# One 7.9 MB load with its last 16 rows taken as sixteen one-row loads from GpSimd's queue

## The chip, the cores and the metric

The kernel runs on one core of a Trainium2 chip. The metric is the device time of one execution in microseconds (us). Two runs of the kernel before gave 711.76 and 711.79 us, median 711.77.

## What is computed

One decode step of two layers, run twice over the same weights and caches: attention with a residual, then an MLP with a residual, each after a layer norm. In short:

```python
def reference(A_x, A_k_cache, A_v_cache, A_wq, A_wo, B_x, B_w1, B_w2):
    x = A_x                                   # 4 x 1 x 640
    for _ in range(2):
        x = x + _A_ref(_layernorm(x), A_k_cache, A_v_cache, A_wq, A_wo)
        x = x + _B_ref(_layernorm(x), B_w1, B_w2)
    return x
```

`_A_ref` is attention with 32 heads of 128 over the last 1024 positions of the caches: q = x wq, softmax of q k / sqrt(128), the weighted sum of v, then wo. `_B_ref` is relu(x w1) w2 with 1728 hidden columns. The batch is 4, with one token each. Everything is float32.

## The kernel before, in words

All weights and caches are read from memory in both rounds (r = 0 and r = 1 in the code), some 302 MB in all, and hardly any of it is used twice. So the host packs the input into rows that are read in long runs. For each of the 32 heads there is a record of REC = 9472 columns over 128 partitions: 640 columns of wq (WQ), 4096 of K, 4096 of V and 640 of wo (WO). Row p of the array `rec` holds the records of all heads one after another, so a load of any stretch of columns is 128 long runs, one for each partition.

On the chip the tile `slots` holds NS = 5 records side by side, and `ring` holds the weights of the MLP and one more record. In round one the heads run in order, and head h lies in slot h % 5.

The order of the loads is written out by hand. `items` (from line 174) lists every load with its source columns and its place. `stream` (line 191) takes the records of five heads as one stretch and cuts it in three, at the columns of CUTS (line 55): 0, 15744, 31616 and 47360. `pump` (line 247) issues the next loads of the list on SP's queue, as long as the columns that they overwrite have been given free; `done` (line 278) gives columns free once the matmuls that read them have been written down, and calls `pump`. The waits on the chip follow from that: a load waits on the last matmul that reads the old content. Each engine's instructions are kept in the order of the program by `InOrder` (line 80).

For head h of round one the program runs: `scores` of the next head on TensorE (PE), `softmax` on VectorE (DVE) and ScalarE (ACT), `values` of this head (PE), `picks` (DVE), `query` of the head after the next (PE), `output_T` and `project` of this head (PE and ACT), `weights` (DVE). The loop stands at lines 512 to 531.

The load that the change touches is the second cut of the group of heads 10 to 14. Its first part is named ("rec", 0, 11). It holds head 11 from its column 6272 on (the rest of V, and WO), all of head 12, and head 13 up to its column 3200 (wq and part of K). It is 15872 columns wide, 63,488 bytes a row. The load before it in the list is the first cut of the same group, the one after it the third cut, and then follows the first cut of heads 15 to 19.

GpSimd (POOL) runs a few instructions that set up constants at the start, and nothing after. ACT issues the four small loads of x at the start (line 141); all other loads are issued by SP.

Of the kernel before, what the change touches and what calls it, by code (L numbers as in the profile page):

```python
# [2 lines left out]

# [11 lines left out]
P = 128  # L40
# [34 lines left out]
W1_SLOT = [[0, 1], [2], [3], [4]]  # L75
W2_SLOT = [22, 14, 10, 4, 4]
LATE = 5


class InOrder:  # L80
# [21 lines left out]
def decode_kernel(ctx: ExitStack, tc: tile.TileContext, xf, rec, w, out):  # L102
    nc = tc.nc
    pe, dve, act, pool, sp = (InOrder(tc, e) for e in (nc.tensor, nc.vector, nc.scalar, nc.gpsimd, nc.sync))
# [11 lines left out]
    hT = scratch.rearrange("p (m j) -> p m j", j=32)  # L116
    oTs = sb.tile([P, LATE, B], F32, name="oTs")
    qT = sb.tile([P, B], F32, name="qT")
# [59 lines left out]
    buffers = {"slots": slots, "ring": ring}  # L178
# [8 lines left out]
    def piece(r, h, lo, hi, buf=None, col=None):  # L187
        buf, col = place(home(h, r) if buf is None else buf, lo if col is None else col)
        items.append(([(("rec", r, h), lo, hi, col)], rec, h * REC + lo, h * REC + hi, buf, col))
# [9 lines left out]
    def ending(r, hs, late):  # L199
# [4 lines left out]
        if late:  # L204
            for h in hs[-1:] + hs[-LATE:-1]:
                piece(r, h, WO, REC)
# [8 lines left out]
    for h in hs[5 * NS:-3]:  # L215
        piece(0, h, 0, RING if h == SIXTH else WO if h >= H - LATE else REC)
    piece(0, SIXTH, RING, REC, "ring", 0)
# [29 lines left out]
    def pump():  # L247

        while items:
            parts, src, lo, hi, buf, col = items[0]  # L250
            if any(b == buf and x < col + hi - lo and col < y for b, x, y in live):
                return
            sp.dma_start(buffers[buf][:, col:col + hi - lo], src[:, lo:hi])
            live.append((buf, col, col + hi - lo))
            for key, x, y, c in parts:
                at.setdefault(key, []).append((x, y, buf, c))
            items.pop(0)
# [20 lines left out]
    def done(key, lo, hi):  # L278

        if key[0] == "rec" and key[1] == 0 and key[2] >= LAST:  # L280
            return
        if key == ("rec", 0, SIXTH):
            hi = min(hi, HELD)
        for x, y, buf, col in pieces(key):
            a, b = col + max(lo, x) - x, col + min(hi, y) - x
            if a < b:
                free(buf, a, b)
        pump()
# [5 lines left out]
    def put_by():  # L294

        for col, a, b in held:
            dve.tensor_copy(hold[:, col:col + b - a], ring[:, a:b])
            free("ring", a, b)
        free("ring", BESIDE, KEPT)
        pump()  # L300

    def lend():

        act.activation(*lent, AF.Copy)
        free("ring", HELD, BESIDE)
        pump()
# [193 lines left out]
    for r in range(2):  # L500
        hs = order[r]
        late = LATE if r == 0 else 2
        if r == 0:
# [8 lines left out]
        for n, h in enumerate(hs[:-2]):  # L512
            i = n - (H - late)
# [82 lines left out]
```

## Time and profile before

| | us |
|---|---|
| median of two runs | 711.77 |
| the profiled execution, its own span | 710.5 |
| PE busy | 513.6 (72%) |
| DVE busy | 323.3 (46%) |
| ACT busy | 99.7 (14%) |
| GpSimd busy | 1.1 |
| share of the 16 DMA engines' span that SP's queue fills | 99.1% |
| mean rate of the DMA | 426 GB/s |

The profile is of one execution. PE is the matmul unit, PEld its weight loads, SP the engine that issues the loads; "SPq" and "ACTq" are the issuing instructions. "slots<-rec" is a load from the array `rec` into the tile `slots`, "acc", "o_ps" and "sc_ps" are tiles in PSUM that matmuls write. A helper (line 94) issues nearly every instruction, so groups are told apart by their tiles and not by their lines. In the parts on the DMA, a packet is one run of bytes that one DMA engine moves, or one completion mark of 4 bytes; a stretch of time counts a packet whole where it starts, so that the share of a short stretch can be over 100%. The queue q1 is SP's, q10 is ACT's; those called "instruction" fetch the program. A row of the chain of waits has its start, its length, and what it is.

### The profile page before, as it was taken

Reading aid. Unit: us, or ns where it says so; the run is one execution under the profiler, and the core shown is the slowest. Engines: PE = TensorE matmul, PEld = TensorE weight load, DVE = VectorE, ACT = ScalarE, POOL = GpSimd, SP = SyncE. Lnnn points to the kernel's source line nnn. Section 1 sums busy time; section 2 is a strip of 40 time slices with the busy share of each in tenths; the row PEclk is TensorE's granted clock in tenths of the full one; section 3 lists DMA queues with packets and bytes.
Section 4 is the critical chain, followed back from the end, with each engine's and each line's share of the span. In section 5 each row is a group of like instructions: output and inputs, shape, how many; then the busy total and the mean of one; then the engine's idle time right before and its main releaser. Section 6 shows DMA issues by size and latency. Waiting matters only on the chain.

```text
span 710.5 us, 8690 instructions
## 1 busy us (share of the span) xinstructions
PE 513.6 (72%) x3706; PEld 202.8 (29%) x3706; DVE 323.3 (46%) x678; ACT 99.7 (14%) x211; POOL 1.1 (0%) x9
## 2 busy tenths in 40 slices
PE   3567686678584578857888898865686677576897
PEld 2132232232231223322223334331331322231423
DVE  3333353353452353546641777644352444253762
ACT  1100110011010110111121212201010111011111
POOL 0000000000000000000000000000000000000000
PEclk9957787677777776888999899977576677677899
DMA  9999999999999999999999999999999999999997
GB/s 381 463 409 451 415 442 443 414 442 444 424 429 440 434 429 421 435 425 430 424 416 403 421 435 428 438 434 448 429 445 427 428 442 430 427 442 406 431 423 292
DMA packets 13318, 302.64 MB, mean 426 GB/s; under 512 B 1488, under 2 KB 1760, under 8 KB 5216
## 3 DMA queue, kind: packets, MB, share of 16 engines
q1 hardware_dynamic: 13248, 302.08, 99.1%
q8 instruction: 29, 0.48, 0.2%
q14 instruction: 9, 0.07, 0.0%
q10 hardware_dynamic: 32, 0.01, 0.0%
HBM read 302.00 MB, written 0.08 MB: 425 GB/s over the span
## 4 chain that ended last, share of the span: by engine, by line
DMA 73%; PE 21%; DVE 4%; issue 1%; ACT 1%; SPq 0%; ACTq 0%; DVEq 0%
DMA slots<-rec 57%; PE sc_ps L94 11%; DMA ring<-w 8%; PE o_ps L94 7%; DMA ring<-rec 5%; PE acc L94 2%; DMA slots<-w 2%; DVE scratch L94 2%; DVE o_ps L94 1%; ACT oTs L94 1%; DVE small L94 0%; ACT sc_ps L94 0%; DVE turned L94 0%; SPq L94 0%; DVE ring L94 0%
## 5 line engine op out<-in xcount | busy, mean ns | idle before, releaser
L94 PE MATMUL sc_ps<-slots,qT 128*4 128x512 f32 x992 | 194.5, 869 | 37.4 <-DMA slots<-rec 36.4
L94 PE MATMUL sc_ps<-xT,slots 128*128 128x4 f32 x620 | 94.6, 279 | 99.8 <-DMA slots<-rec 99.2
L94 PE MATMUL o_ps<-slots,scratch 128*16 128x512 f32 x960 | 149.3, 693 | 2.4 <-DVE scratch L94 1.7
L94 DVE TENSOR_REDUCE small<-sc_ps 128x1 f32<-128x1024 f32 x64 | 78.3, 1224 | 156.9 <-PE sc_ps L94 156.9
L94 PEld LDWEIGHTS sc_ps<-xT,slots 128*128 128x128 f32 x620 | 89.2, 225 | 157.8 <-DMA slots<-rec 109.0
L94 ACT ACTIVATE sc_ps<-sc_ps,small 128x1024 f32<-128x1024 f32 (+1 forms) x68 | 71.1, 1046 | 342.2 <-DVE small L94 340.7
L94 DVE STREAM_TRANSPOSE turned<-sc_ps 128x1024 f32<-128x1024 f32 (+1 forms) x85 | 84.6, 996 | 0.7
L94 PEld LDWEIGHTS o_ps<-slots,scratch 128*16 128x16 f32 x960 | 34.5, 118 | 120.0 <-issue 107.6
L94 DVE TENSOR_TENSOR o_ps<-o_ps,of_block 128x512 f32<-128x512 f32 x62 | 43.4, 699 | 53.6 <-PE o_ps L94 52.3
L94 PEld LDWEIGHTS sc_ps<-slots,qT 128*4 128x4 f32 x992 | 32.3, 108 | 121.9 <-issue 64.9
L94 DVE TENSOR_TENSOR qT<-sc_ps,by_row 128x4 f32<-128x4 f32 x62 | 9.7, 156 | 114.1 <-PE sc_ps L94 114.1
L94 PE MATMUL acc<-slots,oTs 128*4 128x160 f32 x496 | 35.4, 368 | 19.2 <-ACT oTs L94 18.5
L94 DVE TENSOR_REDUCE scratch<-o_ps 128x128 f32<-128x512 f32 x62 | 42.9, 691 | 2.1
L94 ACT ACTIVATE oTs<-o_ps 128x4 f32<-128x4 f32 x64 | 11.1, 174 | 214.1 <-PE o_ps L94 214.1
L94 PE MATMUL o_ps<-pick,scratch 128*128 128x4 f32 x128 | 26.8, 280 | 15.9 <-DVE scratch L94 15.9
L94 PEld LDWEIGHTS o_ps<-pick,scratch 128*128 128x128 f32 x128 | 22.4, 218 | 21.4 <-DVE scratch L94 21.1
L94 DVE TENSOR_TENSOR scratch<-turned,by_row 128x128 f32<-128x128 f32 (+1 forms) x85 | 22.0, 259 | 3.2
L94 PE MATMUL sc_ps<-slots,small 128*1 128x512 f32 (+2 forms) x56 | 21.5, 486 | 0.0
L94 DVE TENSOR_SCALAR by_row<-of_batch,small 128x4 f32<-128x4 f32 x64 | 14.7, 230 | 2.2
L94 PEld LDWEIGHTS acc<-slots,oTs 128*4 128x4 f32 x496 | 6.9, 84 | 25.2 <-ACT oTs L94 23.5
L94 DVE STREAM_TRANSPOSE scratch<-small 128x32 f32<-128x32 f32 x64 | 12.9, 202 | 2.2 <-ACT sc_ps L94 2.2
L94 ACT ACTIVATION_READ_ACCUMULATOR sc_ps<-sc_ps,small 128x1 f32 x64 | 12.3, 193 | 0.0
(66 smaller groups left out, 103.7 us busy)
## 6 DMA issues: line engine op xcount, KB each, us to landing
slots<-rec SPq DMA_DIRECT2D x15, 7872.0 KB, 27.0
slots<-rec SPq DMA_DIRECT2D x8, 7936.0 KB, 31.5
slots<-rec SPq DMA_DIRECT2D x17, 2368.0 KB, 16.9
slots<-rec SPq DMA_DIRECT2D x4, 4736.0 KB, 25.9
slots<-rec SPq DMA_DIRECT2D x2, 4416.0 KB, 29.3
slots<-rec SPq DMA_DIRECT2D x7, 1024.0 KB, 19.7
ring<-w SPq DMA_DIRECT2D x8, 864.0 KB, 10.9
ring<-rec SPq DMA_DIRECT2D x1, 4576.0 KB, 36.2
```

Of the source, the lines that this page charges most:

```text
L94: r = build(*args, **kwargs)
```

## The change

Where `pump` meets the load whose first part is ("rec", 0, 11) and which is wider than ONE = 15733 columns, it issues it in three kinds of pieces: on SP rows 0 to 111 over all 15872 columns, on SP the last 139 columns of rows 112 to 127, and on GpSimd the first 15733 columns of each of the rows 112 to 127, one load a row. All other loads stay. The scratch that is set aside for loads issued by GpSimd grows from 64 to 256 bytes a partition.

```diff
@@
 LATE = 5
+SINGLE = ("rec", 0, 11)
+ONE = 15733
@@ def pump():
             parts, src, lo, hi, buf, col = items[0]
             if any(b == buf and x < col + hi - lo and col < y for b, x, y in live):
                 return
-            sp.dma_start(buffers[buf][:, col:col + hi - lo], src[:, lo:hi])
+            dst = buffers[buf][:, col:col + hi - lo]
+            if parts and parts[0][0] == SINGLE and hi - lo > ONE:
+                sp.dma_start(dst[:P - 16], src[:P - 16, lo:hi])
+                sp.dma_start(dst[P - 16:, ONE:], src[P - 16:, lo + ONE:hi])
+                for i in range(P - 16, P):
+                    pool.dma_start(dst[i:i + 1, :ONE], src[i:i + 1, lo:lo + ONE])
+            else:
+                sp.dma_start(dst, src[:, lo:hi])
             live.append((buf, col, col + hi - lo))
@@ def kernel(...):
-    nc = bacc.Bacc("TRN2", target_bir_lowering=False, num_devices=1, dynamic_dma_scratch_size=64)
+    nc = bacc.Bacc("TRN2", target_bir_lowering=False, num_devices=1, dynamic_dma_scratch_size=256)
```

## The prediction

> **What bounds the kernel now.** I read the page first, then the chain around the changed load, then the DMA rows of short windows.
>
> ```profile
> span 710.5 us, 8690 instructions
> PE 513.6 (72%) x3706; PEld 202.8 (29%) x3706; DVE 323.3 (46%) x678; ACT 99.7 (14%) x211; POOL 1.1 (0%) x9
> ...
> q1 hardware_dynamic: 13248, 302.08, 99.1%
> ...
> DMA 73%; PE 21%; DVE 4%; issue 1%; ACT 1%; SPq 0%; ACTq 0%; DVEq 0%
> ```
>
> The queue of SP (q1) fills 99.1% of all 16 DMA engines' span. PE is busy 72%, but the chain that ended last is 73% DMA. So the kernel ends when 302 MB are in, and a change in the order of transfers costs time only where an engine runs dry or works twice. By the same line it can win at most 0.9% of 710.5, 6.4 us, part of which is the start and the end.
>
> The changed load is the second cut of the group that starts with head 10: columns 15744 to 31616, 15872 columns or 63,488 bytes a row, 7936 KB. It holds the end of head 11, all of head 12 and the start of head 13. The chain in order of time finds it:
>
> ```profile
> 123.91 0.50 PE acc L94 x8
> 124.41 0.02 issue
> 124.42 29.17 DMA slots<-rec
> 153.59 0.04 issue
> 153.63 2.30 PE sc_ps L94 x10
> ...
> 157.40 3.41 PE sc_ps L94 x16
> 160.81 1.70 PE o_ps L94 x7
> 162.51 0.02 issue
> 162.53 28.46 DMA slots<-rec
> ```
>
> The load is issued at 124.42, when the projection of head 7 (PE acc) has freed the columns. It is complete at 153.59. There the query of head 12 has been waiting for it, and 8.94 us of PE work later (up to the values of head 11) the next load is released, at 162.53. One more load stands between the two: the third cut, issued at 146.60.
>
> ```profile
> 146.09 0.46 PE L94 MATMUL acc<-slots,oTs 128*4 128x160 f32 x8 [0.32 <-ACT oTs L94]
> ...
> 146.60 0.33 SPq L94 DMA_DIRECT2D slots<-rec  x1
> ...
> slots<-rec SPq DMA_DIRECT2D x1, 7872.0 KB, 25.6
> ```
>
> It lands at 146.60 + 25.6 = 172.2 and is what keeps the engines fed while PE works on the changed load. Two windows, 165 to 170.35 and 170.35 to 172.2, show when each engine is through with it; small packets (under 512 B) are completions:
>
> ```profile
> DMA packets 42, 2.33 MB, mean 436 GB/s; under 512 B 5, under 2 KB 5, under 8 KB 5
> ...
> DMA packets 23, 0.70 MB, mean 379 GB/s; under 512 B 11, under 2 KB 11, under 8 KB 11
> ```
>
> 5 + 11 = 16: one completion from each engine, the earliest engines shortly before 170.35, the last at about 172.1. So the engines are up to 1.8 us apart, and a load counts when its slowest engine is done.
>
> **How much lateness is free.** From issue to first packet I read SP's first issue (0.80, in the timeline) against the windows 1.0 to 1.75 and 1.75 to 2.1:
>
> ```profile
> 0.80 0.37 SPq L91 DMA_DIRECT2D slots<-rec  x1
> ...
> 1.48 0.45 POOL L94 TENSOR_SCALAR_AFFINE_SELECT of_batch<-of_batch 128x4 f32<-128x4 f32 x2
> ...
> DMA packets 0, 0.00 MB, mean 0 GB/s; under 512 B 0, under 2 KB 0, under 8 KB 0
> ...
> DMA packets 12, 0.23 MB, mean 650 GB/s; under 512 B 0, under 2 KB 0, under 8 KB 0
> ```
>
> First packets come 0.95 to 1.3 us after the issue, say 1. The load issued at 162.53 could therefore start at 163.5, and the slowest engine runs dry at 172.1. If the changed load lands up to 8.6 us later than 153.59, the slowest engine loses nothing; past that, each us is lost. (The earliest engine has 6.7 us, but it has 1.8 us in hand.) Nothing else hangs on it: the issue at 146.60 is released by the projection of head 9 (the PE row at 146.09 above), which needs no column of this load.
>
> **The change part by part.**
>
> Bytes: the same. SP takes rows 0 to 111 whole and the last 139 columns of the other 16 rows; GpSimd takes 16 x 62,932 B, 1.0 of 8.1 MB. One row's time comes from the window 104.2 to 104.3, in which one row of 62,976 B starts:
>
> ```profile
> q1 hardware_dynamic: 1, 0.06, 145.2%
> ```
>
> 145.2% of 16 engines over 0.1 us is 2.32 us. The old load is 8 rows an engine, 18.7 us; the new one 7 on SP's queue (16.4) and, if each one-row load goes to another engine, 1 on GpSimd's (2.3). Sum of bytes: 0.
>
> SP: one issue more, 0.33 us by the row above, at 124.8. Its next issue is 21.8 us later, which covers it. Cost 0; without that cover 0.33.
>
> GpSimd: 16 issues behind the same release as SP's. Its 9 instructions of before end with the two at 1.48 above, so nothing is queued behind its wait. The scratch grows from 64 to 256 bytes a partition, and no instruction with it.
>
> Turns on an engine: the only place where a second queue works beside SP's is the start, where ACT issues four loads of four rows of 640 B while SP's rows of 18,944 B (0.70 us each, by bytes) are queued. The issues, the wait they end in, and the window 4.7 to 9.4:
>
> ```profile
> 1.13 0.56 ACTq L91 DMA_DIRECT2D scratch<-xf  x1
> ...
> 1.72 1.28 ACTq L94 DMA_DIRECT2D scratch<-xf  x3
> ...
> 9.79 0.87 PE L91 MATMUL acc<-scratch,ring 128*128 128x160 f32 x2 [9.79 <-DMA scratch<-xf]
> ```
>
> ```profile
> q1 hardware_dynamic: 125, 2.06, 102.4%
> q10 hardware_dynamic: 32, 0.01, 0.9%
> ```
>
> This is the row that prices the change. 32 packets are 16 rows and 16 completions, 8 packets on each of four engines, spread over 4.6 us: one per 0.66 us, about the length of one SP row, though the packets themselves filled 0.9% x 16 x 4.7 / 32 = 0.02 us each. So an engine takes one packet of each queue in turn, and a completion waits a turn like a row. 10 KB took until 9.8 us. The window up to 4.7 holds no packet of q10:
>
> ```profile
> q1 hardware_dynamic: 51, 0.97, 60.7%
> ```
>
> So the first waited 3.6 us from its issue, 1 of it start-up: three or four SP rows.
>
> Extra packets: at most 17 an engine of 0.02 us that carry no new byte: 0.2 us after the 1.0 MB is left out.
>
> Landing of the 16 rows: a turn now costs an SP row of 2.32 us. The bounds come from the two kinds of load that were counted.
> - Few completions: ACT's loads of four rows posted four each, so a one-row load posts one. From issue it waits 3 rows (7.0), moves its row (2.3), lets one SP row pass (2.3): 11.6 us. At about 1 us an issue (an estimate: ACT's took 0.43 to 0.56, and GpSimd's are not in the trace) and with at most eight in flight before a counter must come back, the ninth goes at 136, the last at 143, and lands at 154.6: 1 us late, 7.6 under what is free. Loss 0.
> - Many completions: SP's loads post 16. If each of the 16 one-row loads posts on every engine, each engine has 17 turns. 3 SP rows pass first, then 16 SP packets, of which four are short (three completions and the 556 B row): 15 rows, 34.9 us, plus its own 2.3 and 1 of start-up. Landing at 162.7, 9.1 late; some ten further semaphores for PE to pass, 0.05 us each as an estimate from the 0.02 to 0.04 us issue steps of the chain: 0.5. Loss 9.6 - 8.6 = 1.0.
> - Far end: GpSimd's issues at 2 us each, with the eight counters on top, put the last row 6 us later: loss 7.
>
> I take the second, 1.0: the dearer of the two counted kinds, since a count of GpSimd's is in no row. The Trainium skill (DMA: Bandwidth & Descriptors, "Why a DMA increments its semaphore by 16 and not by 1") says that loads issued by GpSimd post on all 16 engines whatever their shape, and that few-row loads of the other queues post only where they carry data. The q10 row agrees with its second half; by its first half the sum is the second case, by the q10 row alone it is 0.
>
> Sum: 0 + 0 + 0.2 + 1.0 = 1.2 us on the profiled 710.5. The runs' median is 711.77, 1.3 above that execution, so 713.0. A measurement of this kernel tells about 2%, 14.2 us, from no change: the boundary is 726.0.
>
> **The rivals.**
>
> *Engines collide on their way into the rows (slower, about 730).* In before every load has 128 rows and each engine keeps to eight of them; all rows take 2.32 us, so the trace cannot tell whether an engine or the way into its eight rows sets that rate. After, seven rows an engine cut across the old groups, and 16 engines send rows into the last 16 partitions. If the way is the limit, two engines that meet go at half speed. Lower end: 12 of 16 ways still take 8 rows, so SP's part needs 18.7 and not 16.4: 2.3 us. Upper end: all seven rows at half speed, 16.4, and four guest rows on each of four ways, 9.3: 25.7. A load counts by its slowest engine, which speaks for the upper part: 18 us, 730. It decides as soon as the way has no room to spare. For it: no packet of a row beats 27.1 GB/s. Against: nothing in the trace shows two engines in one way. The Trainium skill (SBUF — State Buffer, "Door 1: The DMA port swizzle") counts 16 ports of eight partitions and says that bandwidth goes by the ports reached; no run here shows it yet. Chance 0.27, of which 0.24 past 726.
>
> *The rows land much later (716 to 722).* The far end above: GpSimd is slow to issue, PE starts on head 12 at 165 or later and the engines run dry for 4 to 10 us. Against it: nothing else runs on GpSimd. Chance 0.15.
>
> *A small gain (710 to 711.5).* The engines end apart:
>
> ```profile
> 700.00:706.00 6.00, 5.10 (x100) 2.85 (x96) 0.87 (x2) 1.08 (x3) 0.00 (x0) 1.00 0.81 332
> ```
>
> From 700 to 706 their share is 0.81, 1.1 us of idle. A pause after the changed load would bring them level, and part of that could come back. Against it: later fetches part them again. Chance 0.05.
>
> *It does not do what it says (711.8 to 712).* If a one-row load is cut over many engines after all, or its rows go ahead of SP's without turns, it lands early and nothing moves. Against it: 15733 is a prime number, with no divisor to cut by. Chance 0.08.
>
> **How the numbers follow.** The forecast, a stall of 0 to 3 us, has 0.45. Slower by over 2%: 0.24 from the collision and 0.01 from the late landing, 0.25. Faster by over 2% needs 14 us where 6.4 are idle: 0.01. Within 2%: 0.74. The range starts at 710.7, half of the small gain, and reaches into the collision to 734, which leaves out about 0.1 at the top. The likeliest case's own range is 711.8 to 715.
>
> **What would show it.** Right: a new queue with 16 rows of 62,932 B and either 16 or 256 completions; the query of head 12 starts at 155 to 164; q1's rows keep 2.32 us; the next load is issued 0 to 10 us later than 162.53; DMA share from 124 to 205 stays at 0.97 or more. Wrong: rows that take well over 2.32 us in the window 126 to 172 (collision), or a gap of more than 3 us with no packets near 172 (late landing). The count of completions decides between the two landings.

## The result, and the profile after

The changed kernel takes 788.73 us (two runs, 787.24 to 790.22) against 711.77 before: a ratio of 1.1081, with a 95% interval of 1.106 to 1.1102. It is 77 us slower; the forecast was 713.0, with a range to 734.

The page of the changed kernel, its span, the queues of the DMA and the issues of GpSimd:

```profile
span 788.5 us, 8725 instructions
...
DMA  9999999993006999999999999999999999999997
GB/s 388 434 458 414 450 413 394 242 311 141 29 23 256 412 453 419 448 423 420 430 425 420 413 391 430 426 435 430 444 434 430 439 418 445 426 432 416 428 419 296
...
q1 hardware_dynamic: 13264, 301.07, 91.5%
q0 software_dynamic: 512, 1.01, 0.4%
...
slots<-rec POOLq DMA_DIRECT2D x16, 61.5 KB, 42.3
```

The two rows by slices show the whole story in one place. From the eighth slice on the rate falls to 242, 311, 141, 29 and 23 GB/s, and only then recovers; the other slices are much as before. Note that the row of busy shares still says 9 in the slices with 242 and 311 GB/s: the engines are busy, but move a half to three quarters of what they moved before. In the slice with 141 GB/s most of them have run dry, and in those with 29 and 23 GB/s all but one. The new queue q0 has 512 packets for 16 loads.

Where head 12 starts, and when the next load is released (timelines of PE and of SP, then of GpSimd):

```profile
235.37 1.84 PE L71 MATMUL sc_ps<-xT,slots 128*128 128x4 f32 x8 [72.63 <-DMA slots<-rec]
...
244.17 0.35 SPq L71 DMA_DIRECT2D slots<-rec  x1
...
124.70 3.73 POOL L71 DMA_DIRECT2D slots<-rec  x7 [122.77 <-PE acc L71]
138.94 0.52 POOL L71 DMA_DIRECT2D slots<-rec  x1 [10.51 <-issue]
147.67 0.52 POOL L71 DMA_DIRECT2D slots<-rec  x1 [8.22 <-issue]
160.94 0.52 POOL L71 DMA_DIRECT2D slots<-rec  x1 [12.75 <-issue]
172.41 0.52 POOL L71 DMA_DIRECT2D slots<-rec  x1 [10.95 <-issue]
186.86 0.52 POOL L71 DMA_DIRECT2D slots<-rec  x1 [13.93 <-issue]
...
209.82 0.52 POOL L71 DMA_DIRECT2D slots<-rec  x1 [6.45 <-issue]
```

The query of head 12 starts at 235.37 where it was 153.63, 81.7 us later, and PE had waited 72.63 us for a load. The next load goes out at 244.17 for 162.53. GpSimd issues seven loads in a row and then one at a time, 2 to 14 us apart, the last at 209.82. Each later issue waits for a landing: the first load is issued at 124.70 and lands 13.9 us later, at 138.6, and the eighth is issued at 138.94. SP's later issues keep a distance of 73 to 79 us to the kernel before, up to the end.

The windows of the changed kernel (columns: stretch, length, busy time of PE, PEld, DVE, ACT, POOL, granted clock, DMA share, GB/s):

```profile
124.00:146.00 22.00, 5.48 (x40) 1.18 (x33) 3.85 (x5) 1.21 (x2) 4.25 (x8) 0.66 0.99 294
146.00:172.00 26.00, 14.51 (x104) 6.46 (x104) 9.39 (x18) 2.76 (x6) 1.04 (x2) 0.70 1.01 280
172.00:190.00 18.00, 0.00 (x0) 0.00 (x0) 0.00 (x0) 0.00 (x0) 1.04 (x2) 0.50 0.71 266
190.00:205.00 15.00, 0.00 (x0) 0.00 (x0) 0.00 (x0) 0.00 (x0) 1.55 (x3) 0.50 0.07 29
205.00:235.00 30.00, 0.00 (x0) 0.00 (x0) 0.00 (x0) 0.00 (x0) 0.52 (x1) 0.50 0.06 25
```

Two losses are to be seen. From 124 to 172 the share is full and the rate 280 to 294 GB/s, where 434 is the rate of 16 engines that move a 62,976-byte row in 2.32 us. From 190 to 235 the share is 0.06 to 0.07, one engine of sixteen, at 25 to 29 GB/s. One engine works and fifteen wait. The queues in that stretch:

```profile
q0 software_dynamic: 144, 0.69, 3.7%
q1 hardware_dynamic: 13, 0.50, 2.6%
```

0.69 MB are eleven of GpSimd's sixteen rows, and 0.50 MB are eight rows of SP's third cut, which that engine moves in between. In the records of single packets these rows follow one another without a gap, all but the first in 2.32 to 2.33 us, so here the engine never waits for GpSimd to issue.

### The profile page after: what moved, and what is told of

Its sections match the earlier page's. It is cut to its first block, busy times and chain, and to the rows that moved or that the text cites. A ratio compares the mean times of both kernels' runs of the same rounds, so it can differ in the third digit from the quotient of the medians.

```text
span 788.5 us, 8725 instructions
## 1 busy us (share of the span) xinstructions
PE 506.6 (64%) x3706; PEld 203.7 (26%) x3706; DVE 323.3 (41%) x678; ACT 99.6 (13%) x211; POOL 9.5 (1%) x25
## 4 chain that ended last, share of the span: by engine, by line
DMA 64%; PE 20%; issue 11%; DVE 3%; POOL 1%; ACT 1%; SPq 0%; ACTq 0%; DVEq 0%; POOLq 0%
DMA slots<-rec 55%; PE sc_ps L71 11%; PE o_ps L71 7%; DMA ring<-w 7%; PE acc L71 2%; DMA slots<-w 2%; DVE scratch L71 2%; DVE o_ps L71 1%; POOL slots L71 1%; ACT oTs L71 1%; SPq L71 0%; DVE ring L71 0%; ACTq L71 0%; SPq L68 0%; DVEq L71 0%
## 5 line engine op out<-in xcount | busy, mean ns | idle before, releaser
L71 PE MATMUL sc_ps<-slots,qT 128*4 128x512 f32 x992 | 185.3, 841 | 38.0 <-DMA slots<-rec 37.2
L71 PE MATMUL o_ps<-slots,scratch 128*16 128x512 f32 x960 | 145.6, 680 | 1.1 <-DVE scratch L71 0.5
L71 PE MATMUL sc_ps<-ring,xT 128*4 128x432 f32 x80 | 11.4, 657 | 1.9 <-DMA ring<-w 1.9
```

Source lines behind the costliest of these rows:

```text
L71: r = build(*args, **kwargs)
```

## The experiments

After the result the theory (A) was: rows that cross the old groups collide; all one-row loads go to one engine; and each load of GpSimd waits turns behind SP's rows. The rivals were that GpSimd's issue with its small ring is the whole cause (B), or that the collision is (C). Three words recur. A way is, in the theory, the path into one group of eight partitions; a turn is one packet of SP's that a packet of GpSimd's waits for on the same engine; the ring is the room in the scratch for the loads that GpSimd has issued (not the tile `ring`). Edits are against the changed kernel unless said otherwise; each kernel was measured beside the kernel before, which then took 711.75 to 712.01 us.

**Two loads of SP, none of GpSimd (split_sp).**

```diff
                 sp.dma_start(dst[:P - 16], src[:P - 16, lo:hi])
-                sp.dma_start(dst[P - 16:, ONE:], src[P - 16:, lo + ONE:hi])
-                for i in range(P - 16, P):
-                    pool.dma_start(dst[i:i + 1, :ONE], src[i:i + 1, lo:lo + ONE])
+                sp.dma_start(dst[P - 16:], src[P - 16:, lo:hi])
```

> No load from GpSimd at all: SP takes rows 0 to 111 in one load and rows 112 to 127 in a second, same bytes. Theory A (three costs: rows that cross the old groups collide and take 4.2 us each instead of 2.34; all sixteen one-row loads go to one DMA engine; every load of GpSimd waits turns behind SP's rows): only the collision is left, 7 rows at 4.2 us and then 16 rows on a quarter of the ways, about 29 + 9 us instead of 18.7, so 728 to 736 us. Rival B (GpSimd's issue with its small ring is the whole cause): 711 to 714. Rival C (the collision is the whole cause): 780 or more.

Measured 738.71 us, ratio 1.0374 (1.0358 to 1.0389). Dividing the rows alone costs 27 us, a little more than A said and far from B and C. Its window 135 to 160:

```profile
DMA packets 103, 6.29 MB, mean 251 GB/s; under 512 B 4, under 2 KB 4, under 8 KB 4
...
q1 hardware_dynamic: 103, 6.29, 101.7%
```

99 rows filled 101.7% of 16 engines for 25 us: 4.11 us a row, where one took 2.32 in the kernel before. No second queue is at work here.

**One load of 16 rows from GpSimd (pool16).**

```diff
-                for i in range(P - 16, P):
-                    pool.dma_start(dst[i:i + 1, :ONE], src[i:i + 1, lo:lo + ONE])
+                pool.dma_start(dst[P - 16:, :ONE], src[P - 16:, lo:lo + ONE])
```

> The sixteen one-row loads become one load of 16 rows from GpSimd, same bytes and same queue. Theory A: one load spreads over 16 engines and costs two turns, so what is left is the collision, 725 to 737 us. Rival B (anything issued by GpSimd is slow): 750 or more. Rival C: 780 or more.

Measured 739.16 us, 1.0384 (1.035 to 1.0417): like two loads of SP, and 2 us past the end of what A allowed. One load on GpSimd's queue adds nothing that these intervals tell from zero. The window 128 to 134.6, in which its rows start:

```profile
q0 software_dynamic: 16, 1.01, 126.7%
```

126.7% x 16 x 6.6 / 16 = 8.4 us a row: sixteen engines write into the last 16 partitions at about a quarter of the speed.

**One-row loads that can be cut (spread).**

```diff
-ONE = 15733
+ONE = 15728
```

> The one-row loads take 15728 columns instead of 15733, a number that 16 divides, so that each can be cut over 16 engines; still sixteen loads from GpSimd with the same ring. Theory A: the single engine's line of 16 rows is gone, turns and collision stay, 735 to 760 us. Rival B (the ring and the turns alone): no change, 780 to 795. If the one-engine line were of no weight: 780 to 795 as well.

Measured 758.37 us, 1.0648 (1.0632 to 1.0663), 30 us less than with the prime number. With 15728 = 16 x 983 each row comes as 16 pieces (256 packets of 3932 bytes). So the one engine is a cause of its own; B and C fall. What is left over the one load of 16 rows is 19 us, and GpSimd's timeline shows how the loads come:

```profile
125.38 3.50 POOL L71 DMA_DIRECT2D slots<-rec  x7 [123.45 <-PE acc L71]
137.53 0.48 POOL L71 DMA_DIRECT2D slots<-rec  x1 [8.66 <-issue]
142.50 0.48 POOL L71 DMA_DIRECT2D slots<-rec  x1 [4.49 <-issue]
151.72 0.48 POOL L71 DMA_DIRECT2D slots<-rec  x1 [8.73 <-issue]
160.75 0.48 POOL L71 DMA_DIRECT2D slots<-rec  x1 [8.55 <-issue]
170.63 0.48 POOL L71 DMA_DIRECT2D slots<-rec  x1 [9.40 <-issue]
```

Seven loads fit. After the eighth, one step is 5.0 us and three are 9 to 10; the last four loads, issued from 173.23 to 186.60, follow at 1 to 6 us.

**One-row loads of 508 bytes (short_rows).** SP loads all columns but the first 127 on all 128 rows, and these 127 on 112 rows.

```diff
-ONE = 15733
+ONE = 127
...
-                sp.dma_start(dst[:P - 16], src[:P - 16, lo:hi])
-                sp.dma_start(dst[P - 16:, ONE:], src[P - 16:, lo + ONE:hi])
+                sp.dma_start(dst[:, ONE:], src[:, lo + ONE:hi])
+                sp.dma_start(dst[:P - 16, :ONE], src[:P - 16, lo:lo + ONE])
```

> GpSimd still issues sixteen one-row loads, but of 127 columns (508 bytes); SP takes all other columns on all 128 rows, and the 127 columns of rows 0 to 111. So there is no long row from GpSimd and hardly a collision; the turns and the ring stay. Theory A: 32 turns on each engine behind SP rows of 2.34 us, landing 30 to 50 us late, 725 to 750 us. Rival C (collision) and a rival by which only the bytes on one engine count: 711 to 715.

Measured 716.24 us, 1.0056 (1.004 to 1.0073). This run does not price what it was made for. Theory A had expected 725 to 750. But the 127 columns take the place of columns that come free earlier, so GpSimd began at 106.5, 18 us before SP's part, and PE's timeline shows no added wait for these rows. GpSimd's timeline shows the turns undisturbed:

```profile
118.86 0.52 POOL L71 DMA_DIRECT2D slots<-rec  x1 [1.81 <-issue]
123.53 0.52 POOL L71 DMA_DIRECT2D slots<-rec  x1 [4.15 <-issue]
128.19 0.52 POOL L71 DMA_DIRECT2D slots<-rec  x1 [4.14 <-issue]
133.01 0.52 POOL L71 DMA_DIRECT2D slots<-rec  x1 [4.30 <-issue]
135.69 0.52 POOL L71 DMA_DIRECT2D slots<-rec  x1 [2.17 <-issue]
140.02 0.52 POOL L71 DMA_DIRECT2D slots<-rec  x1 [3.81 <-issue]
144.68 0.52 POOL L71 DMA_DIRECT2D slots<-rec  x1 [4.14 <-issue]
149.35 0.52 POOL L71 DMA_DIRECT2D slots<-rec  x1 [4.15 <-issue]
```

Five of the seven steps are 4.7 to 4.8 us, two of SP's rows of 2.32: a load of GpSimd puts two packets on each engine (512 packets are 16 loads x 16 engines x 2), and each waits one row. In spread, where SP's rows of this load took some 4.4 us, three steps were 9 to 10.

**Two halves, SP alone (halves).**

```diff
-                sp.dma_start(dst[:P - 16], src[:P - 16, lo:hi])
-                sp.dma_start(dst[P - 16:, ONE:], src[P - 16:, lo + ONE:hi])
-                for i in range(P - 16, P):
-                    pool.dma_start(dst[i:i + 1, :ONE], src[i:i + 1, lo:lo + ONE])
+                sp.dma_start(dst[:64], src[:64, lo:hi])
+                sp.dma_start(dst[64:], src[64:, lo:hi])
```

> Only SP, no GpSimd: the load is cut in rows 0 to 63 and rows 64 to 127, two loads one after the other. If the way into the rows is the limit (16 ways of eight partitions, one engine's rate each), each half reaches 8 ways, two engines share each, and every row takes twice 2.34 us: 37 us instead of 18.7, so 728 to 734 us. If the loss of the earlier splits came from the number 112 or from a second load as such: 711 to 715.

Measured 738.56 us, 1.0367 (1.0352 to 1.0383). It is not the number 112: 64 and 64 rows lose as much. Its rows took the twofold time that was expected: from 136 to 160, 77 rows filled 98.3% of 16 engines, 4.90 us a row. So the way into the rows is the limit, though 5 us more was lost than the upper end of what was expected; the control below explains 3.4 of them.

**The one-row loads issued by SP (sp_rows).**

```diff
-                    pool.dma_start(dst[i:i + 1, :ONE], src[i:i + 1, lo:lo + ONE])
+                    sp.dma_start(dst[i:i + 1, :ONE], src[i:i + 1, lo:lo + ONE])
```

> The sixteen one-row loads are issued by SP instead of GpSimd, so there is no ring of GpSimd and no second queue to take turns with. Theory A (a load of one uncut row goes whole to one engine, and always to the same one): 16 rows in a line on one engine after the 112-row load, 37 us more on it, and SP's next load late behind eight counters: 750 to 770 us. If single rows were dealt over the engines: like the split into two SP loads, 730 to 740. If GpSimd's turns are what costs: at most 740.

Measured 774.41 us, 1.088 (1.0854 to 1.0906), 4 us above what A said. In this program SP's loads count their landings on eight counters in turn, so an issue waits for the load eight before it (the one at 137.19 went out once the load issued at 104.40 had landed); the steps of its timeline are the time of one load:

```profile
168.21 0.22 SPq L71 DMA_DIRECT2D slots<-rec  x1
...
170.53 0.22 SPq L71 DMA_DIRECT2D slots<-rec  x1
...
172.84 0.22 SPq L71 DMA_DIRECT2D slots<-rec  x1
...
175.09 0.22 SPq L71 DMA_DIRECT2D slots<-rec  x1
...
184.44 0.36 SPq L71 DMA_DIRECT2D slots<-rec  x1
```

2.3 us a load, one row after the other on one engine, with no GpSimd in it: from 165 to 184 SP's queue fills 6.9% of the 16 engines, about one engine. The third cut, issued at 146.60 before, had to wait behind them until 184.44, so part of this kernel's loss is that queue and not the line of rows itself.

**Seven rows from GpSimd, nine in one load of SP (seven).**

```diff
-                for i in range(P - 16, P):
+                sp.dma_start(dst[P - 16:P - 7, :ONE], src[P - 16:P - 7, lo:lo + ONE])
+                for i in range(P - 7, P):
                     pool.dma_start(dst[i:i + 1, :ONE], src[i:i + 1, lo:lo + ONE])
```

> GpSimd takes only seven of the sixteen rows as one-row loads, which its ring holds at once; SP takes the other nine in one load. Theory A: no load of GpSimd waits for the ring, but its seven rows stand in a line on one engine, each with two turns; the collision stays at 20 to 27 us and the line adds 5 to 20: 740 to 758 us. If the ring is what costs beyond the collision: 736 to 741, as with two SP loads.

Measured 763.35 us, 1.0716 (1.07 to 1.0732), above the range of A. All seven were issued within 4 us, so no load waited for the ring, and still they cost 25 us over two loads of SP: 3.5 us a row. In the changed kernel the sixteen cost 50 us over it, 3.1 a row. The full ring is not what costs; the line on one engine is, with its turns. SP's part is held by it too: the last row to land was one of SP's nine, moved from 200.31 to 202.63, right behind GpSimd's last, and the query of head 12 started at 203.44.

**An eighth of the columns from GpSimd (pool_cols).**

```diff
-                sp.dma_start(dst[:P - 16], src[:P - 16, lo:hi])
-                sp.dma_start(dst[P - 16:, ONE:], src[P - 16:, lo + ONE:hi])
-                for i in range(P - 16, P):
-                    pool.dma_start(dst[i:i + 1, :ONE], src[i:i + 1, lo:lo + ONE])
+                sp.dma_start(dst[:, :13888], src[:, lo:lo + 13888])
+                pool.dma_start(dst[:, 13888:], src[:, lo + 13888:hi])
```

> GpSimd takes an eighth of the load by columns and not by rows: the last 1984 columns of all 128 rows in one load, SP the rest on 128 rows. Same bytes from GpSimd (1.0 MB), no row pattern that crosses the old groups, one load. Theory A (rows, engines and turns cost, not the queue): 711 to 714 us. If GpSimd's queue itself costs: 720 or more.

Measured 716.02 us, 1.0056 (1.004 to 1.0072). The same bytes on the same queue, by columns over all 128 rows, lose 4 us instead of 77. The comparison is not quite even: these columns come free earlier, so GpSimd's load was issued at 111.01, 13 us before SP's, and landed at 137.7. By the same 26.6 us from issue to landing it would have been in at 151 with SP's release (an estimate), still before the 154.13 at which head 12's query started. The 4 us, 2 above the expectation, were the same as with the short rows, and asked for a control.

**The scratch alone (scratch256, scratch128).** Against the kernel before, with no load of GpSimd:

```diff
-dynamic_dma_scratch_size=64
+dynamic_dma_scratch_size=256
```

> The kernel before with one number changed: the scratch set aside for GpSimd's loads is 256 bytes a partition and not 64, with no load from GpSimd. Both runs in which GpSimd's part should have cost nothing came out 4 us slow, and in every kernel with the larger scratch the rows of all loads took some 0.2 to 0.5% longer (18,944 B: 0.714 us for 0.711). Theory: every tile lies 192 bytes further on, and that costs 3 to 4 us over 302 MB: 715 to 716 us. Rival (a first load from GpSimd costs 4 us by itself): 711.5 to 712.5.

> The kernel before with a scratch of 128 bytes, so that all tiles lie 64 bytes further on. If the place of the tiles matters, this one differs from 711.8, either way by up to 4 us (710 to 716); if only the size of the scratch matters, it lies between 711.8 and the one with 256.

Measured 715.24 us, 1.0046 (1.0033 to 1.0059), and 715.09 us, 1.0045 (1.0032 to 1.0058). So the scratch costs 3.4 us with no load from GpSimd, and a first load from GpSimd at most about 1. 64 bytes more cost as much as 192, so the loss does not grow with the size; that it is the place of the tiles fits, but was not tried in another way (a filler tile, say), and the cause stays open. In the window 10 to 270 the kernel before and the one with 256 moved:

```profile
DMA packets 2172, 113.00 MB, mean 435 GB/s; under 512 B 240, under 2 KB 240, under 8 KB 240
...
DMA packets 2167, 112.68 MB, mean 433 GB/s; under 512 B 240, under 2 KB 240, under 8 KB 240
```

In the records of single packets the loss looks like a fixed 2 to 3 ns a row more than a share of it: the median row took 2.326 us for 2.324 at 62,976 bytes, and 0.707 for 0.705 at 18,944.

**112 rows only (only112).** Rows 112 to 127 of this load are left out.

```diff
                 sp.dma_start(dst[:P - 16], src[:P - 16, lo:hi])
-                sp.dma_start(dst[P - 16:, ONE:], src[P - 16:, lo + ONE:hi])
-                for i in range(P - 16, P):
-                    pool.dma_start(dst[i:i + 1, :ONE], src[i:i + 1, lo:lo + ONE])
```

> SP loads rows 0 to 111 and rows 112 to 127 of this load are left out (they keep what lay there, so the output is not the reference's). It parts the collision in two. Theory: 112 rows dealt seven to an engine take 4.2 us a row, 29 us where 18.7 went before, so with the 4 us of the larger scratch 724 to 729 us, and the 16 rows by themselves (9 us, four engines to one way) make up the rest to 739. Rival (all of the loss is in the 16 rows): 711 to 715.

Measured 727.77 us, 1.0224 (1.021 to 1.0238): with an eighth of the load missing it is 12.5 us slower than the control. The 16 rows as a second load make the other 10.9 up to 738.7.

**Four loads of four rows (rows4).**

```diff
-                for i in range(P - 16, P):
-                    pool.dma_start(dst[i:i + 1, :ONE], src[i:i + 1, lo:lo + ONE])
+                for i in range(P - 16, P, 4):
+                    pool.dma_start(dst[i:i + 4, :ONE], src[i:i + 4, lo:lo + ONE])
```

> GpSimd takes the sixteen rows as four loads of four rows. Theory (a load of k rows goes to k engines, and to the same ones each time): four rows in a line on each of four engines, the ring not full, 742 to 752 us. Rival (each load goes on to the next engines): one row on each engine as in the one load of 16 rows, 737 to 742 us.

Measured 771.92 us, 1.0819 (1.0787 to 1.0851), 20 us past what was expected. All four loads were issued by 127.4. GpSimd's queue in the windows 129 to 132, 132 to 145, 145 to 151, 151 to 163, 163 to 166, 166 to 181 and 181 to 185:

```profile
q0 software_dynamic: 16, 0.25, 75.9%
...
q0 software_dynamic: 27, 0.00, 0.4%
...
q0 software_dynamic: 19, 0.25, 36.3%
...
q0 software_dynamic: 28, 0.00, 0.4%
...
q0 software_dynamic: 14, 0.25, 68.0%
...
q0 software_dynamic: 16, 0.00, 0.2%
...
q0 software_dynamic: 4, 0.25, 57.2%
```

0.25 MB is one load of four rows. They come one load at a time, the first rows of two loads 16 to 18 us apart. On four other engines the second load would have had only two turns of some 5 us before it and would have started by about 140 (an estimate); from 132 to 145 no row starts. So the next four rows wait for the same four engines, and every load of four rows took these, as the theory had it. What it had missed is that four neighbouring rows also share one way, so each row took some 9 us (the last line: 57.2% x 16 x 4 / 4 = 9.2) and held its engine for as long.

**The sum.** Each step changes one thing in the code (medians in us):

| kernel | median | added |
|---|---|---|
| before | 711.8 | |
| scratch of 256 bytes | 715.2 | 3.4 |
| 112 rows, seven an engine | 727.8 | 12.5 |
| the 16 rows as a load of their own | 738.7 | 10.9 |
| the 16 rows as sixteen loads, from SP | 774.4 | 35.7 |
| the sixteen loads from GpSimd | 788.7 | 14.3 |

The shares hold for this order, and one step can hold more than one cost: the 35.7 contain the late issue of the third cut that the counters force. By the other path, sixteen loads from GpSimd in place of one cost 19 us (758.4 - 739.2), put down to their turns, and the one engine then 30 (788.7 - 758.4).

## Why the prediction was wrong

What the prediction read of the kernel before held: the kernel ends when the bytes are in, the query of head 12 waits on this load, and lateness past some 8 us is lost. 81.7 us late less the 8.6 that were free is 73; 77 were lost, 3.4 of them to the scratch. (The slowest engine's last packet of the third cut started at 171.8 and not at 172.1, so 8.3 were free; that changes nothing here.) The failures are in how late the rows came.

- *"if each one-row load goes to another engine ... Sum of bytes: 0."* This is the step that failed most. The condition was set down and not priced. All sixteen rows went through one engine, and from 190 to 235 one engine of sixteen worked. That line with the turns in it is 50 us of the 77 (788.7 - 738.7). A row that could have warned was there, and the prediction read it so: all four loads of x together kept to four engines, 8 packets on each.
- *The collision* had a chance of 0.27 and a price of 18 us. It is real: 12.5 + 10.9 = 23.4 us, inside the bounds of 2.3 to 25.7 that were worked out. Rows took 4.1 to 4.2 us, and 8.4 where sixteen engines shared the ways into the last 16 partitions. The argument for it (a load counts by its slowest engine) was right; that no row showed two engines in one way was taken as evidence against it, which it was not. The Trainium skill (SBUF — State Buffer, "Door 1: The DMA port swizzle") says that the rate goes by how many of 16 ports of eight partitions a load reaches, and that partitions 0 to 63 reach eight of them. The rows of halves (4.90 us for 2.32) and of pool16 (8.4) agree, and its rule deserved more than 0.27.
- *Many completions: 17 turns an engine.* The direction was right, and the count was half. 512 packets are 32 on each engine, two for each load. The Trainium skill's statement that such loads post on all 16 engines (DMA: Bandwidth & Descriptors, "Why a DMA increments its semaphore by 16 and not by 1") agrees with that count. Turns of one SP row each, read from q10, are confirmed by the steps of 4.7 us of short_rows. What was left out is that turns delay SP's rows as well: *"Nothing else hangs on it"* took the loads around this one as untouched, but the first cut of the group landed so late that the query of head 11 started at 147.16 for 134.94, and the third cut was issued at 159.37 for 146.60. No run prices this by itself.
- *At most eight in flight, an issue of about 1 us.* Seven fitted, and an issue took 0.52 us. Neither mattered much: with seven rows and no wait for the ring, a row cost 3.5 us, with sixteen 3.1.
- *The scratch, "and no instruction with it."* Priced at nothing; it cost 3.4 us, for a reason that stays open.
- *The small gain* and *"It does not do what it says"* did not come. The late landing (716 to 722) was right in kind and far too small, since its far end still had the rows on different engines.

Of the signs named ahead, the query's start (235 for 155 to 164), the row's time (4.2 for 2.32), the next load (81.6 us later for 0 to 10) and the share from 124 to 205 (0.77 for 0.97) all said wrong; the count of completions said that the dearer case holds, and more.

## What to carry to other kernels

Where a load is cut by rows, ask first which engine each row goes to and which rows it writes beside whom: the same 8 MB cost 4 us by columns over 128 rows, 27 by rows in two loads, 77 by single rows (each with the 3.4 of the scratch in it). An assumption on which a zero rests ("if each goes to another engine") needs a price for the case that it fails. And a busy share of 1.0 is no sign of health: read the GB/s beside it.

## What the runs showed of the hardware that was not expected

A load of one uncut row went to the same engine each time, from GpSimd (with seven in flight, only one row moved at a time) and, as far as its steps of 2.3 us tell, from SP; the four loads of four rows went to the same four engines. A row of 15728 columns, which 16 divides, came in 16 pieces; one of 15733, a prime number, came whole. With a scratch of 256 bytes seven loads of GpSimd fitted at once, whether of one row on one engine or of 16 pieces. And a scratch larger by 64 or by 192 bytes cost this kernel 0.45%, 3.4 us over 302 MB, without a load that used it.
